# Padding the second score product of an attention kernel from 64 to 128 rows

## The chip, the cores and the metric

The kernel runs on one core of a Trainium2 chip. The metric is the device time of one execution in microseconds (us), shown as the median of several runs. The engines are TensorE (PE for its matrix products, PEld for the loads of its stationary operand), VectorE (DVE), ScalarE (ACT), GpSimd (POOL) and SyncE (SP, which starts the DMAs).

## What is computed

The reference has three stages: a recurrence over 768 time steps for 4 x 8 heads of width 40, a mixing block with a hidden layer of 1280, and a mixture of four attention experts over the 320 features. The change lies in the last stage alone. Cut to what matters:

```python
for e in range(E):                       # 4 experts, for each of 4 batches
    q = x @ wq[e]                        # x: (768, 320), q, k, v: (768, 64)
    k = x @ wk[e]
    v = x @ wv[e]
    scores = scale * (q @ k.transpose(0, 2, 1))
    scores = np.where(causal, -1000000000.0, scores)
    scores = scores - scores.max(-1, keepdims=True)
    a = np.exp(scores)
    a /= a.sum(-1, keepdims=True) + 1e-09
    ye = a @ v @ wo[e]
    # ye is weighted by the expert's gate where it is among the top two, and added up
```

## The kernel before

`tile_kernel` calls `recurrence`, twice `channel_mix`, and then `attention`. Within `attention` (L687) three generators share the engines: `values(b)` makes the values and the gates of a batch, `scores(b, e)` makes the unnormalised attention of one expert, and `outputs(b, pr)` transposes it and multiplies it with the values and `wo`, for two experts at a time. The strings in `ORDER` (L682) fix by hand how the steps of the three are interleaved (v, f and b); a scheduler then places the instructions on each engine, and each engine runs its own in that fixed order.

Most products are made in a number format of 32 bits that one pass of TensorE handles but that carries fewer digits (`F32R`). To keep full precision, operands are split into an upper and a lower part, and several products are added up in PSUM.

For one batch and expert, `scores` first makes queries and keys together in two halves of 384 positions (L752 to L756, PSUM tile `pq`). From `pq` three ScalarE copies make the upper part of the queries in rows 0 to 63 of `Q2` (L757), and the upper part of the keys twice, in both halves of `KH` (L758, L759). VectorE makes the lower part of the queries, in rows 64 to 127 of `Q2` (L760), and the lower part of the keys, `KL`, which has 64 rows only (L762).

Then for each of six blocks of 128 queries a strip of scores is made, 128 to 768 columns wide because of the causal mask, in pieces of at most 512 columns. Each piece takes two products into the same PSUM tile `ps`: L777 multiplies all 128 rows of `Q2` with `KH`, so that upper and lower part of the queries meet the upper part of the keys at once. L778 then adds the upper part of the queries (rows 0 to 63 of `Q2`) times `KL`. So L777 contracts over 128 rows and L778 over 64:

```python
nc.tensor.matmul(ps[:, s0:s1], Q2[:, q], KH[:, s0:s1], start=True, stop=False)
nc.tensor.matmul(ps[:, s0:s1], Q2[:64, q], KL[:, s0:s1], start=False, stop=True)
```

VectorE adds the mask and takes the maximum (L780), ScalarE takes the exponential (L782), GpSimd scales the rows (L801). The PSUM tiles of the strips up to 512 columns have two buffers (tag `s0`), the wider ones one buffer (`s1`); the next user of a buffer waits for ScalarE's exponential. On the other side, L818 transposes the attention blocks, L822 and L824 copy them out on ScalarE and VectorE in turn, L831 multiplies them with the values on 64 columns of the array, and L843 to L845 make the output rows.

In the trace a `64*128` in the shape of an instruction of TensorE means 64 rows and 128 columns of the array; `128*128` is the whole array.

Of the kernel before, what the change touches and what calls it, by code (L numbers as in the profile page):

```python
# [11 lines left out]
F32 = mybir.dt.float32  # L12
F32R = mybir.dt.float32r
# [3 lines left out]
OP = mybir.AluOpType  # L17
# [5 lines left out]
B, H, S, D = 4, 8, 768, 40  # L23
# [663 lines left out]
def attention(tc, pool, vpool, pp, W, ident, X2, X2S, out):  # L687

    nc = tc.nc
# [5 lines left out]
    VS, GT, OT, ST = {}, {}, {}, {}  # L695
    vals = vpool.tile([128, 2, NT, nv], F32, tag="x1", name="vals")

    def values(b):

        bp, b2 = divmod(b, 2)  # L700
        V = VS[b] = vals[:, b % 2]
        OT[b] = [pool.tile([128, 2, S], F32R, tag=nm, name=f"{nm}{b}") for nm in ("oh", "ol")]
        lg = pool.tile([128, NT, E_], F32, tag="lg", name=f"lg{b}")
        for i in range(NT):
            q = slice(128 * i, 128 * i + 128)
            pv = pp.tile([128, nv + E_], F32, tag="m", bufs=2, name=f"pv{b}_{i}")
            for ft in range(2):
                nc.tensor.matmul(pv, X2[bp][:, ft, 0, b2, q], VG[:, ft, 0], start=ft == 0, stop=False)
                nc.tensor.matmul(pv, X2[bp][:, ft, 1, b2, q], VG[:, ft, 0], start=False, stop=False)
                nc.tensor.matmul(pv, X2[bp][:, ft, 0, b2, q], VG[:, ft, 1], start=False, stop=False)  # L710
            for k in range(2):
                nc.tensor.matmul(pv, X2S[bp][:, b2, q], VG[:, 2, k], start=False, stop=k == 1)
            nc.scalar.activation(V[:, i], pv[:, :nv], AF.Copy)
            nc.vector.tensor_copy(lg[:, i], pv[:, nv:])
            if i < NT - 1:
                yield

        rank = pool.tile([128, NT, E_], F32, tag="rank", name=f"rank{b}")
        cmp = pool.tile([128, NT, E_], F32, tag="cmp", name=f"cmp{b}")
        nc.vector.memset(rank, 0.0)  # L720
        for f in range(E_):
            for sl, op in ((slice(0, f), OP.is_gt), (slice(f + 1, E_), OP.is_ge)):
                w = sl.stop - sl.start
                if w:
                    nc.vector.tensor_tensor(cmp[:, :, sl], lg[:, :, f:f + 1].to_broadcast([128, NT, w]),
                                            lg[:, :, sl], op=op)
                    nc.vector.tensor_tensor(rank[:, :, sl], rank[:, :, sl], cmp[:, :, sl], op=OP.add)
        m1 = pool.tile([128, NT], F32, tag="m1", name=f"m1{b}")
        nc.vector.reduce_max(m1, lg, axis=AX.X)
        nc.vector.tensor_tensor(lg, lg, m1[:, :, None].to_broadcast([128, NT, E_]), op=OP.subtract)  # L730
        gt = GT[b] = pool.tile([128, NT, E_], F32, tag="gt", bufs=2, name=f"gt{b}")
        nc.scalar.activation(gt, lg, AF.Exp)
        nc.vector.scalar_tensor_tensor(gt, rank, 1.5, gt, op0=OP.is_lt, op1=OP.mult)
        nc.vector.reduce_sum(m1, gt, axis=AX.X)
        nc.vector.tensor_scalar(m1, m1, 1e-9, None, op0=OP.add)
        nc.vector.reciprocal(m1, m1)
        nc.vector.tensor_tensor(gt, gt, m1[:, :, None].to_broadcast([128, NT, E_]), op=OP.mult)
        yield

    def scores(b, e):  # L740

        bp, b2 = divmod(b, 2)
        n = f"{b}_{e}"
        Q2 = pool.tile([128, S], F32R, tag="q2", bufs=2, name=f"q2_{n}")
        KH = pool.tile([128, S], F32R, tag="kh", bufs=2, name=f"kh{n}")
        KL = pool.tile([64, S], F32R, tag="kl", bufs=2, name=f"kl{n}")
        f = slice(128 * e, 128 * e + 128)
        for hf in range(2):
            q = slice(384 * hf, 384 * hf + 384)
            pq = pp.tile([128, 384], F32, tag="m", bufs=2, name=f"pq{n}_{hf}")  # L750
            for ft in range(2):
                nc.tensor.matmul(pq, QK[:, ft, 0, f], X2[bp][:, ft, 0, b2, q], start=ft == 0, stop=False)  # L752
                nc.tensor.matmul(pq, QK[:, ft, 0, f], X2[bp][:, ft, 1, b2, q], start=False, stop=False)
                nc.tensor.matmul(pq, QK[:, ft, 1, f], X2[bp][:, ft, 0, b2, q], start=False, stop=False)
            for k in range(2):
                nc.tensor.matmul(pq, QK[:, 2, k, f], X2S[bp][:, b2, q], start=False, stop=k == 1)  # L756
            nc.scalar.activation(Q2[:64, q], pq[:64], AF.Copy, scale=scale)  # L757
            nc.scalar.activation(KH[64:, q], pq[64:], AF.Copy)  # L758
            nc.scalar.activation(KH[:64, q], pq[64:], AF.Copy)  # L759
            nc.vector.scalar_tensor_tensor(Q2[64:, q], pq[:64], scale, Q2[:64, q].bitcast(F32), op0=OP.mult,  # L760
                                           op1=OP.subtract)
            nc.vector.tensor_tensor(KL[:, q], pq[64:], KH[64:, q].bitcast(F32), op=OP.subtract)  # L762
            yield
        mx = pool.tile([128, NT], F32, tag="mx", bufs=4, name=f"mx{n}")
        sm = pool.tile([128, NT], F32, tag="sm", bufs=4, name=f"sm{n}")
        P = ST[b, e] = [pool.tile([128, off[i1] - off[i0]], F32, tag=f"P{blk}", bufs=3, name=f"P{n}_{blk}")
                        for blk, (i0, i1) in enumerate(BL)]
        left = [i1 - i0 for i0, i1 in BL]
        for i in range(NT):
            blk = i // 4  # L770
            i0, i1 = BL[blk]
            k = 128 * (i + 1)
            ps = pp.tile([128, 1024 if blk else 512], F32, tag=f"s{blk}", bufs=1 if blk else 2, name=f"ps{n}_{i}")
            q = slice(128 * i, 128 * i + 128)
            for s0 in range(0, k, 512):
                s1 = min(k, s0 + 512)
                nc.tensor.matmul(ps[:, s0:s1], Q2[:, q], KH[:, s0:s1], start=True, stop=False)  # L777
                nc.tensor.matmul(ps[:, s0:s1], Q2[:64, q], KL[:, s0:s1], start=False, stop=True)  # L778

            nc.vector.tensor_tensor_reduce(ps[:, :k], ps[:, :k], neg[:, S - k:], -1.0, 3e38, op0=OP.add,  # L780
                                           op1=OP.min, accum_out=mx[:, i:i + 1])
            nc.scalar.activation(P[blk][:, off[i] - off[i0]:off[i + 1] - off[i0]], ps[:, :k], AF.Exp,  # L782
                                 bias=mx[:, i:i + 1], scale=-1.0, accum_out=sm[:, i:i + 1])
            left[blk] -= 1
            if left[blk]:
                yield
                continue
            m = sm[:, i0:i1]
            nc.vector.tensor_scalar(m, m, 1e-9, None, op0=OP.add)
            nc.vector.reciprocal(m, m)  # L790
            nc.vector.tensor_tensor(m, m, GT[b][:, i0:i1, e], op=OP.mult)  # L791
            for i in range(i0, i1):
                p = P[blk][:, off[i] - off[i0]:off[i + 1] - off[i0]]
                w = 128 * (i + 1)
                if b == B - 1 and e == E_ - 1 and i % 3:
                    if i % 3 == 1:
                        nc.vector.tensor_scalar(p, p, sm[:, i:i + 1], None, op0=OP.mult)
                    else:
                        nc.scalar.activation(p, p, AF.Copy, scale=sm[:, i:i + 1])
                else:  # L800
                    nc.gpsimd.tensor_tensor(p, p, sm[:, i:i + 1].to_broadcast([128, w]), op=OP.mult)  # L801
            yield
# [48 lines left out]
    for n in range(2 * B + 1):  # L851
        b, pr = divmod(n, 2)
        seqs = {"v": chain(*[values(x) for x in (VAL[n] if n in VAL else ())])}
        seqs["f"] = chain(*[scores(b, 2 * pr + r) for r in range(2)]) if n < 2 * B else iter(())
        seqs["b"] = outputs(*divmod(n - 1, 2)) if n else iter(())
        for x in ORDER[n]:
            next(seqs[x], None)
        for x in "vfb":
            for _ in seqs[x]:
                pass  # L860
# [3 lines left out]
def tile_kernel(ctx, tc, ld, vin, rin, U, V, w1, w2, qk, vg, wo, out):  # L864
# [39 lines left out]
    ap = ctx.enter_context(tc.tile_pool(name="ap", bufs=1, reuse_waits="tile"))  # L904
    pp = ctx.enter_context(tc.tile_pool(name="pp", bufs=1, space=PSUM, reuse_waits="tile"))
    attention(tc, ap, xp, pp, AW, ident, X2, X2S, out)


# [27 lines left out]
```

## Time and profile before

| | us |
|---|---|
| median of 3 runs | 997.31 |
| lowest and highest of them | 996.01 and 997.59 |
| the profiled execution, its own time | 994.6 |
| its span, from the first to the last instruction | 992.9 |
| from 723 us to the end of the span: the attention stage | 270.0 |
| TensorE busy in that stage | 259.89 |
| products of L777, and of L778, in that stage | 128 and 128 |

The profile is of one execution. Its time of 994.6 us is 2.7 us under the median of the runs. The three stages follow each other with little overlap; attention starts at about 723 us, with the last product of `channel_mix` (L673) and the first of `values` (L708). Matmuls are pipelined, and their ends are modelled, so the time that one product costs is read from the start of one to the start of the next, and not from its duration.

### The profile page before, as it was taken

The page shows a single profiled execution, that of the slowest core. Times are in us where ns is not written, and L with a number is a line of the kernel's source. Part 1 is how long each engine was busy: PE and PEld are TensorE (multiplying, and loading weights), DVE is VectorE, ACT ScalarE, POOL GpSimd, SP SyncE. Part 2 cuts the span into 40 slices and gives each one's busy share as a digit, 9 for nine tenths or more (in the row PEclk, how much of TensorE's full clock was granted, in tenths as well). Part 3 has the DMA queues.
Part 4 walks back from the last instruction along what each step waited for, and adds up shares of the span by engine and source line. Part 5 has one row for each costly group of instructions (what it writes and reads, how often), then busy time and mean ns, then how long its engine had stood idle before and what let it go on. Part 6 is the DMA issues. An engine that isn't in the chain of part 4 may idle for free.

```text
span 992.9 us, 22271 instructions
## 1 busy us (share of the span) xinstructions
PE 851.0 (86%) x8812; PEld 701.9 (71%) x8812; DVE 668.1 (67%) x1642; ACT 550.6 (55%) x1392; POOL 255.5 (26%) x330
## 2 busy tenths in 40 slices
PE   2553587885897889688999999999999999999997
PEld 2543576785787778577787888878867677777765
DVE  6989897989989868787672323222257756757664
ACT  3785469775876796547442322223157646656563
POOL 7011022311320210245252222012026243234330
PEclk9766579997998999889999999999999999999999
DMA  6432032441342213334110010000000010000001
GB/s 142 97 96 64 8 76 55 108 101 42 82 102 59 54 42 85 101 103 131 59 51 0 11 41 1 1 1 1 1 1 1 1 40 1 7 34 2 27 14 40
DMA packets 57895, 46.80 MB, mean 47 GB/s; under 512 B 45248, under 2 KB 48960, under 8 KB 55872
## 3 DMA queue, kind: packets, MB, share of 16 engines
q1 hardware_dynamic: 57792, 45.38, 17.9%
q8 instruction: 70, 1.15, 0.5%
q14 instruction: 33, 0.27, 0.1%
HBM read 41.44 MB, written 3.93 MB: 46 GB/s over the span
## 4 chain that ended last, share of the span: by engine, by line
PE 49%; DVE 4%; ACT 3%; DMA 3%; issue 1%; SPq 1%; POOL 1%; DVEq 0%; ACTq 0%; POOLq 0%
PE ps L778 4%; PE po L831 4%; PE tp L818 4%; PE ps L777 3%; PE ph L635 3%; PE pa L654 3%; PE pa L653 3%; PE ph L632 3%; PE pa L652 3%; PE ph L633 3%; PE ph L631 3%; DMA ldt<-in_w 2%; PE pa L649 1%; PE pa L648 1%; PE pq L752 1%
## 5 line engine op out<-in xcount | busy, mean ns | idle before, releaser
L801 POOL TENSOR_TENSOR P<-P,sm 128x128 f32<-128x128 f32 (+2 forms) x92 | 82.9, 932 | 162.6 <-DVE sm L791 103.8
L639 DVE SCALAR_TENSOR_TENSOR hl<-ph,hh 128x512 fp32r<-128x512 f32 x60 | 41.1, 690 | 122.4 <-ACT hh L638 121.2
L215 POOL TENSOR_SCALAR_AFFINE_SELECT ga<-ga 64x512 f32<-64x512 f32 x40 | 36.9, 923 | 270.3 <-ACT ga L213 261.1
L276 PE MATMUL pw<-w,tf 32*32 32x40 f32 x1536 | 52.9, 236 | 51.9 <-DVE tf L242 43.4
L638 ACT ACTIVATE hh<-ph 128x512 fp32r<-128x512 f32 x60 | 35.2, 595 | 107.4 <-PE pa L654 96.2
L276 PEld LDWEIGHTS pw<-w,tf 32*32 32x32 f32 x1536 | 48.6, 150 | 56.9 <-issue 32.9
L780 DVE CUSTOM_DVE_ANT_0 ps<-ps,neg 128x640 f32<-128x640 f32 (+4 forms) x96 | 59.8, 637 | 35.4 <-PE ps L778 33.6
L207 ACT ACTIVATE lx<-pg 32x128 f32<-32x128 f32 x192 | 73.3, 382 | 16.3 <-PE pg L200 8.5
L782 ACT ACTIVATE P<-ps,mx 128x640 f32<-128x640 f32 (+4 forms) x96 | 60.5, 633 | 29.6 <-DVE mx L780 16.8
L189 PE MATMUL pb<-ident,bkt 128*128 128x128 f32 x192 | 34.3, 315 | 41.6 <-ACT ga L213 20.7
L279 ACT ACTIVATE uv<-pw 32x320 f32<-32x320 f32 x96 | 41.1, 428 | 51.5 <-PE pw L276 50.0
L233 DVE TENSOR_TENSOR lt<-lt,tmp 128x30 f32<-128x30 f32 (+9 forms) x180 | 63.8, 354 | 3.7
L200 PE MATMUL pg<-ga,bkt 128*128 128x128 f32 x384 | 59.8, 318 | 5.7 <-ACT ga L213 5.4
L231 DVE TENSOR_TENSOR tmp<-lt 128x30 f32<-128x30 f32 (+9 forms) x180 | 61.7, 343 | 3.2
L322 PE MATMUL pn<-rbd,uvt 128*128 128x128 f32 x384 | 62.2, 326 | 1.4 <-ACT uvt L311 1.4
L322 PEld LDWEIGHTS pn<-rbd,uvt 128*128 128x128 f32 x384 | 58.5, 239 | 4.6 <-ACT uvt L311 2.2
L200 PEld LDWEIGHTS pg<-ga,bkt 128*128 128x128 f32 x384 | 56.4, 231 | 6.8 <-ACT ga L213 6.0
L189 PEld LDWEIGHTS pb<-ident,bkt 128*128 128x128 f32 x192 | 23.6, 157 | 48.7 <-ACT ga L213 25.9
L818 PE MATMUL tp<-ident,P 128*128 128x128 f32 x336 | 53.4, 280 | 2.2 <-ACT pt L822 0.8
L822 ACT ACTIVATE pt<-tp 128x128 f32<-128x128 f32 (+1 forms) x64 | 31.4, 490 | 33.9 <-PE tp L818 32.0
L778 PE MATMUL ps<-kl,q 64*128 64x512 f32 (+3 forms) x128 | 49.3, 407 | 0.3
L777 PE MATMUL ps<-kh,q 128*128 128x512 f32 (+3 forms) x128 | 46.6, 387 | 1.1 <-DVE q L760 1.1
(219 smaller groups left out, 2350.7 us busy)
## 6 DMA issues: line engine op xcount, KB each, us to landing
ldt<-in_ld SPq DMA_DIRECT2D x44, 321.6 KB
uv<-in_vin SPq DMA_DIRECT2D x48, 80.0 KB
rbd<-in_rin SPq DMA_DIRECT2D x48, 80.0 KB
rpt<-in_rin SPq DMA_DIRECT2D x48, 80.0 KB
uvt<-in_rin SPq DMA_DIRECT2D x48, 80.0 KB
out<-o SPq DMA_DIRECT2D x24, 160.0 KB
ldt<-in_w SPq DMA_DIRECT2D x4, 512.0 KB
ldt<-in_w SPq DMA_DIRECT2D x5, 320.0 KB
```

What stands on the lines that cost most here:

```text
L200: nc.tensor.matmul(pg[:, p], bkt[:, h * HP + p].rearrange("p k t -> p (k t)"), ga[:, :, h * HP + p], start=True, stop=True)
L207: nc.scalar.activation(LX[g][q, :, x0:x0 + HP].rearrange("p t q -> p q t"), pg[q, :, r, 32 * i:32 * i + 32], AF.Copy)
L231: latest["dve"] = nc.vector.tensor_tensor(tv, L[:, s + 1:, s:s + 1].to_broadcast([128, n, s]), L[:, s:s + 1, :s].to_broadcast([128, n, s]) ...
L233: nc.vector.tensor_tensor(L[:, s + 1:, :s], L[:, s + 1:, :s], tv, op=OP.add)
L276: nc.tensor.matmul(pw[qs[r], p], tf[qs[r], :, uu * PP + p], w0[qs[r], p], start=p == 0, stop=True, skip_group_check=True)
L322: nc.tensor.matmul(pn[:, p], ut[:, h * HP + p].rearrange("p r t -> p (r t)"), rbd[u % 2][:, :, h * HP + p], start=True, stop=True)
L777: nc.tensor.matmul(ps[:, s0:s1], Q2[:, q], KH[:, s0:s1], start=True, stop=False)
L778: nc.tensor.matmul(ps[:, s0:s1], Q2[:64, q], KL[:, s0:s1], start=False, stop=True)
L780: nc.vector.tensor_tensor_reduce(ps[:, :k], ps[:, :k], neg[:, S - k:], -1.0, 3e38, op0=OP.add, op1=OP.min, accum_out=mx[:, i:i + 1])
L782: nc.scalar.activation(P[blk][:, off[i] - off[i0]:off[i + 1] - off[i0]], ps[:, :k], AF.Exp, bias=mx[:, i:i + 1], scale=-1.0, accum_out=sm[ ...
L801: nc.gpsimd.tensor_tensor(p, p, sm[:, i:i + 1].to_broadcast([128, w]), op=OP.mult)
L818: nc.tensor.transpose(pt[:, j - j0], P[:, c:c + 128], ident)
```

## The change

The two tiles for the lower parts of the keys are now made once, with 128 rows, and the upper half of each (rows 64 to 127) is set to zero once by GpSimd. The experts use the two in turn. VectorE writes the lower part of the keys into rows 0 to 63 as before. L778 (L782 in the new numbering) now multiplies all 128 rows of `Q2` with all 128 rows of that tile: rows 64 to 127 meet zeros, and the sum is the same.

```diff
@@ -695,6 +695,10 @@
     vals = vpool.tile([128, 2, NT, nv], F32, tag="x1", name="vals")
 
+    KLS = [pool.tile([128, S], F32R, name=f"kl{i}") for i in range(2)]
+    for t in KLS:
+        nc.gpsimd.memset(t[64:].bitcast(F32), 0.0)
+
     def values(b):
@@ -743,7 +747,7 @@
-        KL = pool.tile([64, S], F32R, tag="kl", bufs=2, name=f"kl{n}")
+        KL = KLS[e % 2]
@@ -759,7 +763,7 @@
-            nc.vector.tensor_tensor(KL[:, q], pq[64:], KH[64:, q].bitcast(F32), op=OP.subtract)
+            nc.vector.tensor_tensor(KL[:64, q], pq[64:], KH[64:, q].bitcast(F32), op=OP.subtract)
@@ -775,7 +779,7 @@
                 nc.tensor.matmul(ps[:, s0:s1], Q2[:, q], KH[:, s0:s1], start=True, stop=False)
-                nc.tensor.matmul(ps[:, s0:s1], Q2[:64, q], KL[:, s0:s1], start=False, stop=True)
+                nc.tensor.matmul(ps[:, s0:s1], Q2[:, q], KL[:, s0:s1], start=False, stop=True)
```

On TensorE, VectorE, ScalarE and SyncE the instructions stand in the same order in both kernels; only line numbers differ (from L698 on, the new ones are higher by 4). GpSimd has two instructions more. This is GpSimd's queue where attention begins, before: L469 is the last step of `channel_mix`, L801 the first scaling of attention rows (`P`).

```order
L469 TENSOR_TENSOR x_1_7324<-t_2_0_8157,x_1_7324 128x2x256 [waits Activation_49]
L469 TENSOR_TENSOR x_1_7324<-t_2_1_8162,x_1_7324 128x2x256 [waits Activation_49]
L801 TENSOR_TENSOR P_0_0_8254<-P_0_0_8254,sm_0_8253 128x128 [waits DVE_49,Activation_49]
L801 TENSOR_TENSOR P_0_0_8254<-P_0_0_8254,sm_0_8253 128x256 [waits Activation_49]
L801 TENSOR_TENSOR P_0_0_8254<-P_0_0_8254,sm_0_8253 128x384 [waits Activation_49]
```

And the same place in the changed kernel:

```order
L469 TENSOR_TENSOR x_1_7324<-t_2_0_8157,x_1_7324 128x2x256 [waits Activation_49]
L469 TENSOR_TENSOR x_1_7324<-t_2_1_8162,x_1_7324 128x2x256 [waits Activation_49]
L700 MEMSET kl_8185 64x768 [waits Pool_49]
L700 MEMSET kl_8186 64x768
L805 TENSOR_TENSOR P_0_0_8257<-P_0_0_8257,sm_0_8256 128x128 [waits DVE_49,Activation_49,Pool_49]
L805 TENSOR_TENSOR P_0_0_8257<-P_0_0_8257,sm_0_8256 128x256 [waits Activation_49]
```

The two fills stand between the last step of the stage before and the first scaling. They wait for GpSimd's own earlier work alone.

This is TensorE's queue where the first products of L778 stand, before (`pv` belongs to `values`, `ps` to the scores; a product's shape names its output alone):

```order
L710 MATMUL pv_1_8230<-vg,x_0_6403 128x260
L712 MATMUL pv_1_8230<-vg,x2s_6404 128x260 x2
L778 MATMUL ps_0_0_8256<-kl_0_8201,q_0_0_8199 128x128
L778 MATMUL ps_0_1_8272<-kl_0_8201,q_0_0_8199 128x256
L777 MATMUL ps_0_4_8341<-kh_0_8200,q_0_0_8199 128x512 [waits DVE_49]
```

And the same place in the changed kernel:

```order
L714 MATMUL pv_1_8233<-vg,x_0_6403 128x260
L716 MATMUL pv_1_8233<-vg,x2s_6404 128x260 x2
L782 MATMUL ps_0_0_8259<-kl_8185,q_0_0_8203 128x128 [waits Pool_49]
L782 MATMUL ps_0_1_8275<-kl_8185,q_0_0_8203 128x256
L781 MATMUL ps_0_4_8344<-kh_0_8204,q_0_0_8203 128x512 [waits DVE_49]
```

No product has moved. The first product that reads each of the two tiles now waits for GpSimd too.

## Rows read from the trace of the kernel before

**Rows 1.** Windows view: the attention stage and two stretches of it.
```profile
core 0: us, PE busy (x) PEld busy (x) DVE busy (x) ACT busy (x) POOL busy (x), PEclk, DMA share, GB/s
723.00:993.00 270.00, 259.89 (x1505) 190.89 (x1505) 174.23 (x563) 159.92 (x401) 87.26 (x96) 1.00 0.05 16
...
747.00:800.00 53.00, 52.69 (x292) 37.29 (x291) 37.88 (x129) 35.70 (x94) 23.89 (x27) 1.00 0.00 1
...
850.00:900.00 50.00, 49.78 (x299) 38.90 (x297) 33.01 (x100) 32.17 (x82) 16.22 (x18) 1.00 0.06 21
```

**Rows 2.** The page's chain that ended last, shares by engine.
```profile
PE 49%; DVE 4%; ACT 3%; DMA 3%; issue 1%; SPq 1%; POOL 1%; DVEq 0%; ACTq 0%; POOLq 0%
```

**Rows 3.** Timeline of PE, 927 to 930: start, us, line, names, rows*columns, shape.
```profile
927.19 0.39 PE L777 MATMUL ps<-kh,q 128*128 128x512 f32 x1
927.51 0.49 PE L778 MATMUL ps<-kl,q 64*128 64x512 f32 x1
927.93 0.38 PE L777 MATMUL ps<-kh,q 128*128 128x256 f32 x1
928.25 0.38 PE L778 MATMUL ps<-kl,q 64*128 64x256 f32 x1
928.56 0.44 PE L777 MATMUL ps<-kh,q 128*128 128x384 f32 x1
928.93 0.44 PE L778 MATMUL ps<-kl,q 64*128 64x384 f32 x1
929.30 0.41 PE L843 MATMUL py<-wo,oh 128*128 128x320 f32 x1
```

**Rows 4.** Timeline of PE, full-array neighbours: channel mix at 700, attention at 910.
```profile
700.46 0.39 PE L653 MATMUL pa<-hl,w 128*128 128x512 f32 x1
...
700.92 0.39 PE L653 MATMUL pa<-hl,w 128*128 128x512 f32 x1
...
910.50 0.34 PE L753 MATMUL pq<-x,qk 128*128 128x384 f32 x1
910.67 0.35 PE L754 MATMUL pq<-x,qk 128*128 128x384 f32 x1
```

**Rows 5.** Timeline of PE, 722 to 724, around the only other 64-row product there.
```profile
722.91 0.44 PE L673 MATMUL pa<-lo,ii 64*64 64x512 f32 x1
723.28 0.39 PE L708 MATMUL pv<-vg,x 128*128 128x260 f32 x1
723.51 0.29 PE L709 MATMUL pv<-vg,x 128*128 128x260 f32 x1
723.63 0.28 PE L710 MATMUL pv<-vg,x 128*128 128x260 f32 x1
```

**Rows 6.** Timeline of PEld, the loads of the stationary operand, at 910 and 927.
```profile
910.50 0.19 PEld L754 LDWEIGHTS pq<-x,qk 128*128 128x128 f32 x1
...
927.51 0.18 PEld L778 LDWEIGHTS ps<-kl,q 64*128 64x128 f32 x1 [0.28 <-issue]
```

**Rows 7.** Source view of L778: duration ns min/median/max, first and last start.
```profile
L778 PE MATMUL ps<-kl,q x128: 322/384/502, 729.9 to 969.1; 64*128 64x512 f32 x48, 64*128 64x128 f32 x32, 64*128 64x256 f32 x32, 64*128 64x384 f32 x16
```

**Rows 8.** GpSimd's last work before attention, a fill, and the first L778 (timelines, lines).
```profile
724.76 2.55 POOL L469 TENSOR_TENSOR x<-t,x 128x512 fp32r<-128x512 f32 x2
...
L140 POOL MEMSET ga<- 64x512 f32 x28 | 14.6, 522 | 1.4
...
729.89 0.49 PE L778 MATMUL ps<-kl,q 64*128 64x128 f32 x2
```

**Rows 9.** Timeline, 747 to 749: an exponential and the product that reuses its buffer.
```profile
747.41 0.47 ACT L782 ACTIVATE P<-ps,mx 128x256 f32<-128x256 f32 x1
...
748.91 0.48 PE L777 MATMUL ps<-kh,q 128*128 128x512 f32 x1
```

**Rows 10.** Windows view, two stretches of the recurrence (columns as in rows 1).
```profile
410.00:413.00 3.00, 0.00 (x0) 0.00 (x0) 2.98 (x14) 2.62 (x9) 0.99 (x1) 0.98 0.25 52
413.00:423.00 10.00, 6.62 (x81) 5.00 (x82) 7.30 (x15) 4.10 (x8) 2.97 (x3) 0.50 0.27 93
```

## The prediction

> **What bounds the kernel now.** I read the windows view of the last stage first, because the change touches nothing earlier. From 723 to 993 us TensorE is busy for 259.89 of 270.00 us, VectorE for 174.23 and ScalarE for 159.92 [rows 1]. The chain that ended last runs mostly over TensorE [rows 2]. So in this stage the start-to-start distances of TensorE's products add up to the time, and what one of them gives back moves the end, until another engine is late.
>
> Then I read TensorE's timeline for what a product costs, by starts. On the full array, neighbours of 512 columns stand two in 0.46 us, so 0.23 us each, and neighbours of 384 columns 0.17 us apart [rows 4]; those of 260 columns stand 0.12 us apart [rows 5]. The score products do not keep to this. At 927.19 six of them, two each of 512, 256 and 384 columns, take 2.11 us up to the start of L843 [rows 3]. At the full-array distances they would take 2 x (0.23 + 0.12 + 0.17) = 1.04 us. The clock is granted in full (1.00, its level of 2.4 GHz) in all these stretches [rows 1], so the clock is not the cause.
>
> Where the excess sits: L777 of 512 columns to L778 takes 0.32 us instead of 0.23, and L778 of 512 columns to the next L777 0.42 instead of 0.23 [rows 3]. In the loads the reason is visible. The load for L754 starts at 910.50, 0.17 us ahead of its product at 910.67 and beside the running L753 [rows 4, 6]. The load for L778 starts at 927.51, together with its own product, after the load unit stood idle for 0.28 us [rows 3, 6]. A second place with other data behaves alike: L673, the one 64-row product before attention, is followed by L708, which takes 0.23 us to its successor where the next two stand 0.12 us apart [rows 5], a load of 0.11 us that was not hidden. So the cost follows the change of shape from 128 to 64 rows and back: the array seems to run empty before the shape changes, and the first product of the new shape shows its load.
>
> **The change, part by part.** *The price of one excursion to 64 rows.* The three in rows 3 cost 2.11 - 1.04 = 1.07 us, and the L843 behind the last shows one more load of 0.11 us [rows 5]: 1.18 / 3 = 0.39 us. It splits into 0.09 for running empty on the way in (0.32 - 0.23), 0.11 for the load of L778, 0.08 to 0.09 for running empty on the way out, and 0.11 for the load of the next product.
>
> *How many.* L778 has 128 products [rows 7]; in 18 cases two stand directly behind each other in TensorE's order, as the first two of all (the x2 at 729.89 [rows 8]). That leaves 110 excursions: 110 x 0.39 = 42.9 us. Nine of them lead into L831, which uses 64 columns and may have a change of shape of its own left; that keeps between nothing and half the price there, 0 to 1.8 us, and I take 0.9. **The sum on TensorE is 42 us.** The least known piece is a product of 128 columns on the full array, 32 of the 128 [rows 7]: continued down from 0.12 us at 260 columns and 0.23 at 512 it would take 0.06 us, and at the most as much as one of 260, 0.12. With 64 such products (L777 and L778) at up to 0.06 us each way, the sum lies between 39 and 45.
>
> *What the padded product costs itself.* It has the same columns, and L777 beside it is a full-array product of the same width with the same stationary operand, so it should take 0.23, 0.17, 0.12 us as those of rows 4 and 5 do. Rows of zeros add no columns. No instruction on TensorE is added or moved.
>
> *The two fills.* GpSimd finishes L469 at 724.76 + 2.55 = 727.31 us, the first L778 starts at 729.89 [rows 8], and no excursion lies before that one, so it does not come earlier. A fill of 64 x 512 takes 522 ns [rows 8], one of 64 x 768 by the same rate 0.78, and two 1.57: done at about 728.9, 1.0 us before they are needed. The first scaling behind them in GpSimd's queue needs a whole strip of scores first. Cost nothing; if fills took twice as long, 0.6 us once.
>
> *What comes late next.* A faster TensorE meets buffers that ScalarE and VectorE free. A place that shows it: the L777 at 748.91 reuses the buffer that the exponential at 747.41 frees at 747.88, 1.03 us earlier [rows 9]. Four excursions lie in the 5.6 us before it, worth 1.6 us, so about 0.5 us of them would turn into a wait: one third. The stretch from 747 to 800 has 26 excursions. Shortened by 10.1 us to 42.9, it holds VectorE's 37.88 us (88%) and ScalarE's 35.70 (83%) [rows 1]: with a fixed order on each engine not all of it will fit. From 850 to 900, 23 excursions leave 41.0 us for 33.01 and 32.17 (81% and 78%) [rows 1], which is looser. I put the third on the first 36 excursions (723 to 800, 14.0 us), giving 4.7, and a twentieth on the other 28 us, giving 1.4: 6 us in all. The ends are nothing, and a third of everything, 14 us.
>
> **The sum.** 42 - 6 = 36 us. The profiled execution took 994.6 us, so the changed one would take 958.6; the median of the runs is 2.7 us above the profiled one, which gives **961 us**, faster by 3.6%.
>
> **The rivals.**
>
> *The waits take a third everywhere* (14 of 42 us): 994.6 - 28 + 2.7 = 969 us. For it speak the loop of rows 9 and the 88% of VectorE; against it the looser stretches behind 800 us.
>
> *The loads stay visible.* Only the running empty would go, 0.17 of the 0.39 us: 110 x 0.17 = 19 us, of which a slower queue gives back about 1, so 994.6 - 18 + 2.7 = 979 us. For it: L777 and L778 keep the same rows 0 to 63 of the array busy, and the load of one has to pass beside the product of the other. Against it: L753 and L754 share all 128 rows, and the load at 910.50 runs beside a product all the same [rows 4, 6]. The Trainium skill, "TensorE: Matmul & The Clock Gate", Part 3, "The mechanism", says that loads overlap with running matmuls only where their row groups differ; by that rule this rival would hold and the time would be 979 us. The trace disagrees with it at the rows just named.
>
> *Nothing changes.* If the extra time belonged to the second product that adds into the same PSUM tile, or to a product of this size as such, padding would leave it: 0 us, 997 us. Against it: L754 adds into the tile of L753 at 0.17 us, and the excess appears at L708 behind L673 too, in another tile [rows 4, 5]. The Trainium skill, same page, "Why this matters for your kernels", says a single product of few rows takes as long as one of 128; by that alone padding gives nothing. No row speaks against it for the products' own streaming; the excess stands between them.
>
> *Slower: the clock falls.* In the recurrence TensorE stood idle from 410 to 413 us, and from 413 to 423 its granted clock was 0.50, the level of 1.2 GHz [rows 10]. If the new waits in attention opened such gaps again and again, each would be followed by products at half rate. At half rate a microsecond of products costs one more, so the change loses once more than 36 us of TensorE's remaining 220 run so; at 45 us the time would be 994.6 - 36 + 45 + 2.7 = 1006 us. Against it: the waits I expect are about half a microsecond, and with the stage's present gaps, 10 us in all, the clock stays at 1.00 [rows 1].
>
> **How the numbers follow.** The forecast has 0.80, the waits 0.09, the visible loads 0.05, nothing 0.03, the clock 0.03. The range takes in the forecast with its bounds (45 gained and nothing lost gives 952; 39 gained and 9 lost gives 967) and the rival of the waits at 969 with a few us beyond: 952 to 973. Left out are the loads, nothing and the clock, 0.11, and the tails. A change under 0.2% is about what a measurement of this kernel cannot tell from none. Faster by more: 0.80 + 0.09 + 0.05 = 0.94; within: 0.03; slower: 0.03.
>
> **What would show it.** In the profile of the changed kernel every score product should read 128*128, a pair of 512 columns should stand 0.23 us apart on both sides, the load for the second product should start before that product, and the product behind it should not show its 0.11 us. TensorE's idle time in the stage should grow by about 6 us, most of it before 800 us, on VectorE's and ScalarE's tiles. The span up to 723 us and the first second-products at 729.9 should stay. I am wrong if those distances stay above 0.3 us, if the load still starts with its product, or if the idle time grows by more than 14 us.

## The result, and the profile after

The changed kernel takes 961.66 us in the median of four runs (959.37 to 964.90) against 996.66 us for the kernel before (four runs now, one more than in the table of the time before): a ratio of 0.9659, with a 95% interval from 0.9620 to 0.9698. The profiled execution took 959.4 us, its span is 957.7 us. The forecast was 961 us in a range from 952 to 973.

The attention stage is what changed. It begins with the first product behind L673, at 723.28 us before [rows 5] and at 722.73 us after, and lasts to the end of the span: 992.9 - 723.28 = 269.6 us before, 957.7 - 722.73 = 234.9 us after. The difference is 34.6 us, nearly all of the 35.2 us between the two profiled executions.

The windows view of the changed kernel, with the columns of rows 1, for the whole stage and for its first dense stretch:

```profile
723.00:958.00 235.00, 223.86 (x1504) 186.71 (x1503) 173.94 (x563) 157.39 (x401) 88.03 (x98) 1.00 0.05 18
...
747.00:790.00 43.00, 42.62 (x286) 35.32 (x285) 35.92 (x124) 32.95 (x90) 21.34 (x24) 1.00 0.00 1
```

TensorE's busy time fell from 259.89 us [rows 1] to 223.86, that of VectorE and ScalarE hardly moved (174.23 and 159.92 before, 173.94 and 157.39 now). TensorE still sets the pace: it is idle for 11.1 of 235 us, against 10.1 of 270. The chain that ended last says so too, for the whole program:

```profile
PE 61%; DVE 16%; ACT 15%; DMA 5%; issue 3%; POOL 1%; SPq 0%; DVEq 0%; ACTq 0%; POOLq 0%
```

This is TensorE's timeline at the same six products as in rows 3 (L781 and L782 are L777 and L778 before):

```profile
899.69 0.39 PE L781 MATMUL ps<-kh,q 128*128 128x512 f32 x1
899.92 0.40 PE L782 MATMUL ps<-kl,q 128*128 128x512 f32 x1
900.15 0.28 PE L781 MATMUL ps<-kh,q 128*128 128x256 f32 x1
900.27 0.28 PE L782 MATMUL ps<-kl,q 128*128 128x256 f32 x1
900.39 0.34 PE L781 MATMUL ps<-kh,q 128*128 128x384 f32 x1
900.56 0.34 PE L782 MATMUL ps<-kl,q 128*128 128x384 f32 x1
900.74 0.31 PE L847 MATMUL py<-wo,oh 128*128 128x320 f32 x1
```

From the first to L847 it is 1.05 us, where rows 3 have 2.11. Each product now takes its columns' time: 0.23, 0.12 and 0.17 us. The loads of the stationary operand at the same place:

```profile
899.69 0.19 PEld L782 LDWEIGHTS ps<-kl,q 128*128 128x128 f32 x1
899.92 0.19 PEld L781 LDWEIGHTS ps<-kh,q 128*128 128x128 f32 x1
900.16 0.19 PEld L782 LDWEIGHTS ps<-kl,q 128*128 128x128 f32 x1
```

The load for the L782 at 899.92 starts at 899.69, beside the product before it. In rows 6 it started together with its own product, behind 0.28 us of idleness.

### The profile page after: what moved, and what is told of

Its sections match the earlier page's. It is cut to its first block, busy times and chain, and to the rows that moved or that the text cites. A ratio compares the mean times of both kernels' runs of the same rounds, so it can differ in the third digit from the quotient of the medians.

```text
span 957.7 us, 22274 instructions
## 1 busy us (share of the span) xinstructions
PE 810.1 (85%) x8812; PEld 692.4 (72%) x8812; DVE 670.5 (70%) x1642; ACT 547.3 (57%) x1392; POOL 256.1 (27%) x332
## 4 chain that ended last, share of the span: by engine, by line
PE 61%; DVE 16%; ACT 15%; DMA 5%; issue 3%; POOL 1%; SPq 0%; DVEq 0%; ACTq 0%; POOLq 0%
PE pn L322 5%; PE po L835 4%; PE pw L276 4%; ACT lx L207 3%; PE tp L822 3%; PE ph L635 3%; PE pa L654 3%; PE ph L632 3%; PE pa L653 3%; PE pa L652 3%; PE ph L633 3%; PE ph L631 3%; DMA ldt<-in_ld 3%; PE ps L782 2%; ACT ga L213 2%
## 5 line engine op out<-in xcount | busy, mean ns | idle before, releaser
L638 ACT ACTIVATE hh<-ph 128x512 fp32r<-128x512 f32 x60 | 35.2, 595 | 107.1 <-PE pa L654 95.9
L200 PE MATMUL pg<-ga,bkt 128*128 128x128 f32 x384 | 55.8, 304 | 5.7 <-ACT ga L213 5.5
L200 PEld LDWEIGHTS pg<-ga,bkt 128*128 128x128 f32 x384 | 52.7, 218 | 6.8 <-ACT ga L213 6.0
L668 POOL TENSOR_TENSOR t<-t,ul 128x512 f32<-128x512 f32 x12 | 15.3, 1295 | 119.9 <-DVE t L667 119.8
L654 PE MATMUL pa<-hh,w 128*128 128x512 f32 x120 | 47.0, 392 | 0.0
L632 PE MATMUL ph<-ul,w 128*128 128x512 f32 x120 | 46.8, 390 | 0.2 <-DVE ul L621 0.2
```

Source lines behind the costliest of these rows:

```text
L200: nc.tensor.matmul(pg[:, p], bkt[:, h * HP + p].rearrange("p k t -> p (k t)"), ga[:, :, h * HP + p], start=True, stop=True)
L632: nc.tensor.matmul(ph, w[:, 0, f], ul[:, ft], start=False, stop=False)
L654: nc.tensor.matmul(pa[ft], w[:, 2 * DM - FT[2][0] + o:2 * DM - FT[2][0] + o + m], hh, start=False, stop=last)
```

## The experiments

The part of the kernel ahead of attention is the same code in all of them but the three that change the mixing block. Its length differs from one profiled execution to the next: attention began at 722.7 us in one (the changed kernel) and at 732.7 in another (the grouped one). The granted clock goes with it: over the first 300 us, in the recurrence, its mean, between the levels of 1.2 and 2.4 GHz, was 0.85 in the first of these and 0.80 in the second. The length of the attention stage hardly does: the changed kernel, profiled a second time, has 234.9 us again. So the table gives that length beside the time, and for the mixing block the length from its first product into `ph` to the first product of attention. Each ratio is to the kernel before as it ran on the same chip, and the experiments of the table ran on two chips.

| kernel | time, us | ratio to before, interval | mixing block, us | attention, us |
|---|---|---|---|---|
| before | 996.66 | | 239.6 | 269.6 |
| changed | 961.66 | 0.9659, 0.9620 to 0.9698 | 239.3 | 234.9 |
| changed, again | 965.11 | 0.9674, 0.9641 to 0.9707 | 239.7 | 234.9 |
| lasting tiles, 64 rows | 1000.67 | 1.0028, 1.0003 to 1.0052 | 239.6 | 269.6 |
| before, grouped | 987.12 | 0.9900, 0.9863 to 0.9938 | 239.8 | 257.5 |
| 96 rows | 965.15 | 0.9686, 0.9645 to 0.9728 | 239.7 | 235.1 |
| excursions in the mixing block, one product | 984.90 | 0.9871, 0.9836 to 0.9906 | 262.4 | 234.9 |
| narrow mixing products, two instead of one | 983.03 | 0.9853, 0.9816 to 0.9891 | 261.6 | 234.8 |
| folding on 128 rows | 963.98 | 0.9657, 0.9625 to 0.9688 | 237.8 | 235.5 |

**The changed kernel again**, to have its time on the chip of the later runs.

> The changed kernel once more, to have its time beside the next two on the same chip: 962 us, within 2, by every theory.

It took 965.11 us, 0.9674 of the kernel before on that chip, 1 us outside what was expected. The stage is the same to a tenth of a microsecond; in the profiled execution all of what is longer lies ahead of it (attention began at 731.16 us instead of 722.73).

**The tiles alone.** Is it the 128 rows, or the way in which the tiles are kept?

```diff
-                nc.tensor.matmul(ps[:, s0:s1], Q2[:, q], KL[:, s0:s1], start=False, stop=True)
+                nc.tensor.matmul(ps[:, s0:s1], Q2[:64, q], KL[:64, s0:s1], start=False, stop=True)
```

> The changed kernel with its two lasting tiles and the two fills, but the second score product on 64 rows again, as before. My theory (the time goes where the array changes between 128 and 64 rows): 110 such excursions are back, so the time is that of the kernel before, 997 us, within 2. Rival (the lasting tiles did it, by fewer waits when a tile is taken up again): 962 us.

The stage is back at 269.6 us. The tiles and fills give nothing; the rows do it all. The time of 1000.67 us is 4 us above the kernel before (0.3%; the interval begins at 1.0003) and 3.7 us above what was expected, a miss of the 2 us allowed. In the profiled execution the difference lies ahead of attention, which began at 727.35 us instead of 723.28, in code that is the same in both.

**Fewer excursions with the same products.** On 64 rows, the kernel before with both products of one kind first:

```diff
                 nc.tensor.matmul(ps[:, s0:s1], Q2[:, q], KH[:, s0:s1], start=True, stop=False)
+            for s0 in range(0, k, 512):
+                s1 = min(k, s0 + 512)
                 nc.tensor.matmul(ps[:, s0:s1], Q2[:64, q], KL[:, s0:s1], start=False, stop=True)
```

> The kernel before, with 64 rows, but where a strip of scores has two pieces, both products on 128 rows are issued first and then both on 64 rows. The number of products on 64 rows stays at 128; the excursions to 64 rows in TensorE's order of attention fall from 110 to 78. My theory (a price for each excursion, 0.32 to 0.39 us): 32 fewer are 10 to 12 us, 985 to 987 us. Rival (a price for each product on 64 rows, or for each second product into the same PSUM tile): no change, 997 us.

987.12 us, and the stage is 12.1 us shorter: 12.1 / 32 = 0.38 us for each excursion that went. All 128 products still use 64 rows. TensorE's timeline shows a strip of two pieces, each kind issued together:

```profile
927.25 0.51 PE L777 MATMUL ps<-kh,q 128*128 128x512 f32 x2
927.69 0.61 PE L780 MATMUL ps<-kl,q 64*128 64x512 f32 x2
928.23 0.44 PE L777 MATMUL ps<-kh,q 128*128 128x384 f32 x1
```

Four products of 512, 256, 512 and 256 columns take 0.98 us here; in rows 3 the like four took 1.37 (927.19 to 928.56). The rival with a price for each narrow product falls.

**96 rows.** What counts as narrow?

```diff
-                nc.tensor.matmul(ps[:, s0:s1], Q2[:, q], KL[:, s0:s1], start=False, stop=True)
+                nc.tensor.matmul(ps[:, s0:s1], Q2[:96, q], KL[:96, s0:s1], start=False, stop=True)
```

> The changed kernel, but the second product reads 96 rows (64 of data and 32 of zeros) instead of 128. The built program names the array's shape for it as 128 x 128, as for a full product. My theory in its form 'the shape of the array decides': 962 us, as the changed kernel. In its form 'any product with fewer rows than the one before pays': 110 excursions are back, 997 us. Rival (only a load of the same rows can be hidden): between, 979 us.

965.15 us, and the stage is 235.1 us, as with 128 rows. The timeline reads 96 rows in the second product, and full distances:

```profile
903.62 0.39 PE L781 MATMUL ps<-kh,q 128*128 128x512 f32 x1
903.84 0.39 PE L782 MATMUL ps<-kl,q 96*128 96x512 f32 x1
904.07 0.28 PE L781 MATMUL ps<-kh,q 128*128 128x256 f32 x1
```

So a number of rows that differs from the neighbour's isn't enough. What fits both is the shape of the array that the program names for the product: 128 x 128 for 96 rows, 64 x 128 for 64. The trace doesn't print that shape, and no other number of rows was tried.

**The price at another place.** Excursions put into the mixing block of the changed kernel, where TensorE hardly ever waits (238.81 us busy from 483 to 723 us):

```diff
             for k in range(2):
-                nc.tensor.matmul(ph, W.w1[fb, 2][:, k, f], us, start=False, stop=k == 1)
+                m = 64 if k else 128
+                nc.tensor.matmul(ph, W.w1[fb, 2][:m, k, f], us[:m], start=False, stop=k == 1)
```

> The changed kernel, with excursions put in at another place: in the mixing block the second of the two products on the last 64 features reads 64 rows instead of 128 (it leaves out the lower parts in that product; 60 products of 512 columns, none of them second in a PSUM tile or first). TensorE is busy all through that block, so nothing covers it. My theory: 60 excursions at 0.39 us are 23 us more than the changed kernel, 985 us (at 0.32 us, the mean that the change gave back in attention, 981 us). Rival (the extra time belonged to the second score product as such): 962 us.

984.90 us. The mixing block grew from 239.3 (239.7 in the second profile) to 262.4 us: 22.7 to 23.1 us, or 0.38 us for each of 60 excursions, while attention kept its 234.9. The timeline of one excursion, with the load unit below it:

```profile
644.06 0.82 PE L636 MATMUL ph<-us,w 128*128 128x512 f32 x2
644.81 0.50 PE L631 MATMUL ph<-uh,w 128*128 128x512 f32 x1
645.14 0.39 PE L632 MATMUL ph<-ul,w 128*128 128x512 f32 x1
...
644.38 0.18 PEld L636 LDWEIGHTS ph<-us,w 64*128 64x128 f32 x1 [0.35 <-issue]
644.81 0.19 PEld L631 LDWEIGHTS ph<-uh,w 128*128 128x128 f32 x1 [0.25 <-issue]
644.92 0.19 PEld L632 LDWEIGHTS ph<-ul,w 128*128 128x128 f32 x1
```

The first product (128 rows) lasts to the start of the second at 644.38, 0.32 us; the second (64 rows) to 644.81, 0.43 us; the L631 behind it to 645.14, 0.33 us. With 0.23 each they exceed by 0.09, 0.20 and 0.10 us: 0.39 in sum. Both the narrow product and the one behind it load with their start; the load of L632 runs ahead again. The signature of rows 3 and 6 is here without a score product, in other data.

**Twice the products, the same excursions:**

```diff
-                nc.tensor.matmul(ph, W.w1[fb, 2][:, k, f], us, start=False, stop=k == 1)
+                nc.tensor.matmul(ph, W.w1[fb, 2][:64, k, f], us[:64], start=False, stop=k == 1)
```

> As the run with excursions in the mixing block, but both products on the last 64 features read 64 rows (it leaves out the lower parts in both). They stand next to each other in TensorE's order, so there are 120 products on 64 rows but still 60 excursions. My theory (a price for each excursion): the same as with one product, about 985 us. Rival (a price for each product on 64 rows): twice as much, 1008 us.

983.03 us; the mixing block has 261.6 us, no more than with one product. In TensorE's order not all of the 120 stand in pairs: there are 36 pairs, 24 single ones and 5 longer groups, and five of these 65 stand right behind an L673, on 64 rows too. With the six of L673 that makes 66 excursions, as many as with one product, and 6 in the changed kernel; so 60 were put in by either kernel. A second narrow product beside a narrow one is free of extra time. The five behind L673 even start together with it:

```profile
664.04 0.44 PE L673 MATMUL pa<-lo,ii 64*64 64x512 f32 x1
664.04 0.49 PE L635 MATMUL ph<-us,w 64*128 64x512 f32 x1
```

L673 reads rows 64 to 127 and these L635 rows 0 to 63. Five times the 0.23 us of 512 columns are 1.2 us, an estimate of what this saves; that the 0.8 us by which the block is shorter than with one product come from it isn't shown.

A pair also shows the parts of an excursion one by one, because the way out lies behind the second product and the visible load behind the first (lines of TensorE's timeline, then one of the load unit's):

```profile
597.11 0.39 PE L654 MATMUL pa<-hh,w 128*128 128x512 f32 x1
597.43 0.49 PE L635 MATMUL ph<-us,w 64*128 64x512 f32 x1
597.76 0.39 PE L635 MATMUL ph<-us,w 64*128 64x512 f32 x1
598.09 0.50 PE L631 MATMUL ph<-uh,w 128*128 128x512 f32 x1
598.42 0.40 PE L632 MATMUL ph<-ul,w 128*128 128x512 f32 x1
...
597.54 0.19 PEld L635 LDWEIGHTS ph<-us,w 64*128 64x128 f32 x1
```

The four distances are 0.32, 0.33, 0.33 and 0.33 us instead of 0.23. The load for the second narrow product starts at 597.54, 0.22 us ahead of it, so the 0.10 us behind that product are the way out alone.

**The last narrow product outside the recurrence:**

```diff
-        nc.scalar.activation(lo[64:], pa[2][64:], AF.Copy)
+        nc.scalar.activation(lo, pa[2], AF.Copy)
...
-        nc.tensor.matmul(pa[2][:64], ii[64:], lo[64:], start=False, stop=True, skip_group_check=True)
+        nc.tensor.matmul(pa[2][:64], ii[1], lo, start=False, stop=True, skip_group_check=True)
```

> The changed kernel with the same remedy at the only other place with a 64-row product outside the recurrence: the six products at the end of the mixing block's pieces that fold the lower half into the upper now use all 128 rows, with zeros in the stationary operand, and ScalarE copies 128 rows instead of 64 in the same instruction. My theory: 6 excursions at 0.39 us are 2.3 us, 959.4 us against the changed kernel's 961.7. Rival (ScalarE or the wait before it sets the pace there): no change, 961.7 us.

(`ii[1]` is a new tile with zeros in rows 0 to 63.) 963.98 us where 959.4 were expected, ratio 0.9657 (0.9625 to 0.9688), beside 965.11 and 0.9674 (0.9641 to 0.9707) for the changed kernel: the intervals overlap, so a gain in time isn't shown. In the trace the mixing block is 1.9 us shorter (237.8 against 239.7), 0.3 us for each of the six, and attention 0.6 us longer (235.5 against 234.9). Product by product, only distances in the first 8 us of attention differ from those of the changed kernel, some longer and some shorter; why was not looked into.

**How much the waits took.** A pair of kernels with less work for VectorE:

```diff
-            nc.vector.tensor_tensor_reduce(ps[:, :k], ps[:, :k], neg[:, S - k:], -1.0, 3e38, op0=OP.add,
+            nc.vector.tensor_tensor_reduce(ps[:, k - 128:k], ps[:, k - 128:k], neg[:, S - 128:], -1.0, 3e38, op0=OP.add,
```

> To weigh the wait term. The changed kernel, but VectorE masks and takes the maximum over the last 128 columns of each strip only (it leaves out the rest of the maximum and of the sign change), so VectorE has about 30 us less to do in attention and frees the score buffers earlier. To be read as the difference of the attention stage (from the first product behind L673 to the end of the span) to its twin on 64 rows. If the new waits take 6 us of the gain, as the forecast had it, the difference grows from the 34.6 us of the full kernels to about 39 to 41. If they take 1 to 2 us and the price of an excursion was set too high, it stays at 35 to 36.5.

> The twin of the run before: the same short maximum, and the second score product on 64 rows. Its attention stage should be close to the full kernel's 269.6 us, since TensorE sets the pace there; the difference to the run before is what tells: 39 to 41 us if waits took 6 us of the gain, 35 to 36.5 if they took 1 to 2.

Each ran once, in 966.53 us (128 rows) and 1004.66 (64 rows). The stages have 237.2 us on 128 rows and 273.3 on 64, a difference of 36.2 us against 34.6 for the full kernels. That is the side of the small wait term. It is no clean measure of it: the scheduler ordered this pair otherwise than the full kernels (112 excursions instead of 110), both got longer instead of shorter, and the one on 128 rows still waits on other engines (what TensorE waited for: us in total, times, longest):

```profile
PE ps L781 <- DVE q L764: 2.7, 4, 1.2
PE ps L781 <- ACT P L786: 1.9, 3, 0.7
```

The first of these lines stands in the profile of the twin on 64 rows as well; the second does not.

## Why the prediction held, point by point

**What bounds the stage: right.** Every microsecond that left TensorE's distances left the time, but for the few that waits took. VectorE and ScalarE did the same work in less time: from 747 to 790 us VectorE is busy for 35.92 of 43 us, 84%.

**Where the excess sits: right.** The way in and the way out cost about 0.09 us each and the two loads 0.10 to 0.11 each; the pair of narrow products in the mixing block shows all four in rows of its own. One thing the prediction read off the wrong row: that the clock was 1.00 around 700 us too doesn't stand in rows 1. The windows view has it:

```profile
483.00:723.00 240.00, 238.67 (x1096) 191.78 (x1095) 83.12 (x137) 67.95 (x123) 49.88 (x52) 1.00 0.05 14
```

The grouped kernel and the one with two products show that the excursion is paid, not the product.

**The price of one excursion: right at the place where it was read, too high as a mean.** Around a product of 512 columns with full-array products on both sides, 0.38 us were measured twice (12.1 / 32 and 22.9 / 60) for the 0.39 of the forecast. But the 110 in attention gave back 34.6 us, 0.31 each; without the 32 that grouping removes, (34.6 - 12.1) / 78 = 0.29. I had multiplied the price of three excursions in wide products with all 110. Three kinds are cheaper. Those of 128 columns leave the load of the next product in sight even on the full array, as at this L756 behind two short products, which takes 0.23 us to its successor instead of 0.17 (TensorE's timeline of the changed kernel):

```profile
893.50 0.22 PE L781 MATMUL ps<-kh,q 128*128 128x128 f32 x1
893.56 0.27 PE L782 MATMUL ps<-kl,q 128*128 128x128 f32 x1
893.67 0.39 PE L756 MATMUL pq<-x,qk 128*128 128x384 f32 x1
893.90 0.34 PE L757 MATMUL pq<-x,qk 128*128 128x384 f32 x1
```

And those that lead into L831 keep most of the way out. Before, a 64-row product of 128 columns took 0.26 us to the start of L831, now the 128-row product takes 0.21 (first the kernel before, then the changed one, with L835 for L831):

```profile
922.96 0.33 PE L778 MATMUL ps<-kl,q 64*128 64x128 f32 x1
923.22 1.08 PE L831 MATMUL po<-pt,vals 128*64 128x512 f32 x4
```

```profile
895.83 0.27 PE L782 MATMUL ps<-kl,q 128*128 128x128 f32 x1
896.04 1.40 PE L835 MATMUL po<-pt,vals 128*64 128x512 f32 x6
```

The third are the 25 that lead into the transposition L818, a product of 128 columns: on it 0.05 us came back in the mean, where the forecast had 0.11 for the load.

Summed over the starts of all 1504 products of the stage, in the same order in both traces, L777 and L778 and the products right behind L778 gave back 35.2 us, and all others lost 0.6. So the term of 42 us, and its lower bound of 39, was too high: 35.2 us, plus what waits took within it. The bounds did not follow from their working either: 64 products at up to 0.06 us are 3.8 us each way, 38 to 46, and 35.2 lies below that too.

**The waits: the mechanism right, the size too high.** The place of rows 9 waits now, as it was to. This is the exponential that frees the buffer and the load that waits for it:

```profile
744.84 0.47 ACT L786 ACTIVATE P<-ps,mx 128x256 f32<-128x256 f32 x1
...
745.45 0.19 PEld L781 LDWEIGHTS ps<-kh,q 128*128 128x128 f32 x1 [0.29 <-ACT P L786]
```

The wait is 0.29 us, where I had 0.5. The exponential itself comes earlier when TensorE does (744.84 instead of 747.41), which I had left out: the buffer's loop runs over TensorE too. I then put that third on the first 36 excursions, 4.7 us, and 6 us in all; TensorE's idle time in the stage grew by 1.0 us (11.1 - 10.1), and the other products lost 0.6 us. Product by product, eleven distances in the stage grew by more than 0.06 us, 1.8 us in sum: 1.0 up to 800 us and 0.8 behind it, against 4.7 and 1.4 in the forecast. The one of this place is the second longest, with 0.29 us. The pair with the light VectorE speaks for 1 to 2 us too. Waits inside distances that shrank all the same aren't in that sum, so what the waits took to the microsecond stays open.

**The sum: 36 us forecast, 34.6 in the stage and 35.0 in the medians.** With 1.8 us of waits, TensorE's term comes to 34.6 + 1.8 = 36.4 us: the forecast had 5.6 us too much there and 4.2 us too much for the waits, and one error took back most of the other. That the sum came so close is luck; the range of 952 to 973 would have held with either error alone (957 or 967 us).

**The fills: right.** 0.78 us each were forecast; the timeline of GpSimd shows both in 1.41 us:

```profile
726.82 1.41 POOL L700 MEMSET kl<- 64x768 f32 x2
```

They end at 728.23 us, and the first product that waits for them starts at 729.24, 1.0 us later, as forecast.

**The rivals.** The visible loads did not come: the load of L782 starts 0.23 us ahead of its product, although both products use the same rows. The rule that would have made this the outcome stands in the Trainium skill's "TensorE: Matmul & The Clock Gate", Part 3, "The mechanism": loads overlap with running matmuls only where the row groups differ, although the same section also names loads into a background weight buffer. These rows are against that rule; between full-array products it does not hold. The rival that nothing changes is refuted by the 34.6 us themselves. Waits of a third, 14 us, are refuted by TensorE's idle time and by the sum of the longer distances. The clock stayed at 1.00 through the dense stretch and the stage.

## What to carry to other kernels

Read what a product costs from start to start, and look at its neighbours: one on 64 rows of the array among products on 128 cost 0.31 us here in the mean beyond its columns, and up to 0.39, for the way there and back. Fewer columns of the array alone need not cost anything, as the next section shows. If such products are scattered among full ones, fill them with zeros to the full array, or put those of one shape next to each other; grouping them took back 12 of the 35 us without any zeros. And before a price read at one place is multiplied with a count, read it at the narrowest case and at each kind of neighbour.

## What the runs showed of the hardware that I had not expected

A product of 96 rows pays nothing: it has the distances of a full one (0.23 us for 512 columns), its load runs ahead, and the stage is as long as with 128 rows (235.1 and 234.9 us). Fewer columns of the array are not like fewer rows either: in the mixing block a product on 128 rows and 64 columns stands between full ones at 0.22 to 0.24 us, their own distance (TensorE's timeline of the changed kernel):

```profile
655.47 0.39 PE L633 MATMUL ph<-uh,w 128*128 128x512 f32 x1
655.69 0.40 PE L649 MATMUL pa<-hl,w 128*64 128x512 f32 x1
655.93 0.39 PE L653 MATMUL pa<-hl,w 128*128 128x512 f32 x1
656.16 0.40 PE L654 MATMUL pa<-hh,w 128*128 128x512 f32 x1
```

Yet L835, on 64 columns too, takes 0.21 us from the product of 128 columns ahead of it, where another full one follows in 0.11 (893.56 to 893.67). What tells the two apart, the place of the columns or the number format of L835, wasn't tried.
